# Splitting a weight load three ways, shifting small tiles and moving residual adds to the matrix engine in a fused attention and MLP forward and backward kernel

## The chip, the cores and the metric

The kernel runs on one core of one Trainium2 chip. The metric is the device time of one execution in microseconds (us). The kernel before took 856.96 us as the median of three runs (855.38 to 858.51). PE is the matrix engine, DVE the vector engine, ACT the scalar engine, POOL GpSimd, and SP the engine whose in-order queue issues the transfers (DMA). "Clock" is the granted clock of PE as a share of full speed.

## The reference, cut to what matters

```python
def reference(A_x, A_wqkv, A_wo, B_w1, B_w3, B_w2, B_x, grad_out):
    # h  = x + linear_attention(layernorm(x)) @ wo;  h2 = h + (silu(n @ w1) * (n @ w3)) @ w2, n = layernorm(h)
    # x: (1, 2048, 640) bf16, 32 heads of 20, hidden width 1728
    ...
    phi = lambda t: jnp.where(t > 0, t + 1, jnp.exp(t)) + 1e-6
    pq, pk = phi(q), phi(k)
    kv = jnp.einsum("bhsd,bhse->bhde", pk, v)
    z = jnp.einsum("bhsd->bhd", pk)
    num = jnp.einsum("bhqd,bhde->bhqe", pq, kv)
    den = jnp.einsum("bhqd,bhd->bhq", pq, z)[..., None] + 1e-6
    o = num / den
    ...
    _out, _vjp = jax.vjp(_f, A_x, A_wqkv, A_wo, B_w1, B_w3, B_w2)
    return (out, *grads)     # the output and six gradients
```

Of the kernel before, what the change touches and what calls it, by code (L numbers as in the profile page):

```python
# [9 lines left out]
P = 128  # L10
# [8 lines left out]
S, D, H, F = 2048, 640, 32, 1728  # L19
# [3 lines left out]
ST, DT, CT = S // P, D // P, CP // P  # L23
FT, FP = 14, 1792
FL = F - 13 * P
W, SC, TPC = 512, 4, 4
# [40 lines left out]
def kernel(  # L67
# [112 lines left out]
    def load_x(a, b):  # L180
        dma(out=x_sb[:, a:b, :], in_=xS[:, a:b, :])
# [35 lines left out]
    def load_pqT(c):  # L217
        dmaT(out=pqT[:, :, c * W:(c + 1) * W], in_=pq_d[c * W:(c + 1) * W, :])
# [15 lines left out]
    def on_act(t):  # L234
        return t >= XT_DMA and t % 2 == 0

    def p1_norm(t):
        xn = x_sb[:, t, :]
        (ln1.norm_act if on_act(t) else ln1.norm)(xn, xn, t)
        if t >= XT_DMA:  # L240
            dmaT(out=pqT[:, :, t * P:(t + 1) * P], in_=xn)

    def p1_tr(t):
        xn = x_sb[:, t, :]
        tr = ps.tile([P, DT, P], BF16, name="tr", bufs=2)
        for c in range(DT):
            T.transpose(tr[:, c, :], xn[:, c * P:(c + 1) * P], ident[:])

        A.copy(out=pqT[:, :, t * P:(t + 1) * P], in_=tr[:])  # L249
# [6 lines left out]
    def p1_mm(t, n0):  # L256
        acc = ps.tile([P, 2, 512], F32, name="big", bufs=2)
        for j in range(2):
            p1_half(acc[:, j, 0:HD], t, n0 + j * HD)
        return acc  # L260
# [6 lines left out]
    def phi(acc, dst, then=None):  # L267

        mq, rq = (p1.tile([P, D], BF16, name=n, bufs=4) for n in ("mq", "rq"))
        A.activation(two(mq[:]), acc[:, :, 0:HD], AF.Exp)  # L270
        A.activation(two(rq[:]), acc[:, :, 0:HD], AF.Relu)

        def rest():
            V.tensor_scalar(out=mq[:], in0=mq[:], scalar1=1.0, scalar2=1e-6, op0=ALU.min, op1=ALU.add)
            V.tensor_tensor(out=dst, in0=mq[:], in1=rq[:], op=ALU.add)
            if then is not None:
                then()
        held.append(rest)

    def phi_rest():  # L280
        while held:
            held.pop(0)()
# [4 lines left out]
    def q_tile(t):  # L287
        pq = p1.tile([P, D], BF16, name="pq", bufs=4)
        phi(p1_mm(t, 0), pq[:], lambda: q_store(t, pq[:]))
# [9 lines left out]
    def ghh_chunk(n, acc):  # L299

        c, fc = divmod(n, FT)
        mm5_to(acc, w2T, fc, g2T[c])
        if n % 2 == 0:
            ghh[n // 2] = pf.tile([P, 2, W], BF16, name="ghh", bufs=4)
        A.copy(out=ghh[n // 2][:, n % 2, :], in_=acc[:])  # L305
# [5 lines left out]
    def m_part(m, tiles):  # L311
        if m not in macc:
            macc[m] = [ps.tile([P, 512], F32, name="macc", tag=("m", "tr")[m % 2], bufs=2) for _ in range(2)]
        for t in tiles:
            for j, n in enumerate((HD, HD + 1)):
                T.matmul(macc[m][j][:, 0:n], lhsT=pk_all[:, t, m * P:(m + 1) * P],  # L316
                         rhs=x_ext[:, t, j * HD:j * HD + n], start=(t == 0), stop=(t == ST - 1))

    def m_end(m):
        mb = mbs[:, m % 4, :]  # L320
        acc = macc.pop(m)
        for j in range(2):
            A.copy(out=mb[:, j * HD:(j + 1) * HD], in_=acc[j][:, 0:HD])
        V.tensor_copy(out=Z[:, m:m + 1], in_=acc[1][:, HD:HD + 1])
        dmaT(out=mT[:, :, m * P:(m + 1) * P], in_=mb)
        dma(out=m_v[:, m, :], in_=mb)

    def kv_block(m, acc):

        a, b = M_H[m]  # L330
        n = (b - a) * DH
        for c in range(DT):
            T.matmul(acc[:, 0:n], lhsT=mT[:, c, m * P:(m + 1) * P],
                     rhs=wqkv[:, c, 2 * D + a * DH:2 * D + b * DH], start=(c == 0), stop=(c == DT - 1))
        kv, mk = (x[:, m, y].rearrange("p (h e) -> p h e", e=DA)
                  for x, y in ((kvbd, slice(a * DA, b * DA)), (mask, slice(0, M_W[m]))))
        V.tensor_tensor(out=kv[:, :, 0:DH], in0=acc[:, 0:n].rearrange("p (h e) -> p h e", e=DH),
                        in1=mk[:, :, 0:DH], op=ALU.mult)
        V.tensor_scalar(out=kv[:, :, DH], in0=mk[:, :, DH], scalar1=Z[:, m:m + 1], scalar2=None, op0=ALU.mult)
# [16 lines left out]
    def load_w2T(a, b):  # L356
        dmaT(out=w2T[:, :, a:b], in_=B_w2[a:b, :])
# [12 lines left out]
    def group_out(g):  # L370
        sl = slice(g * TPC, (g + 1) * TPC)
        dma(out=pk_v[:, sl, :], in_=pk_all[:, sl, :])
        dma(out=xn_v[:, sl, :], in_=x_sb[:, sl, :])

    for t in range(ST):
        g, i = divmod(t, TPC)
        k = p1_mm(t, D)
        if t == 0:
            p1_tr(1)
        for n in stat_of.get(t, ()):  # L380
            ln1.run(x_sb, n, n + 1)
            if on_act(n):
                ln1.bias(n)
        for n in norm_of.get(t, ()):
            if not on_act(n):
                p1_norm(n)
        phi_rest()
        phi(k, pk_all[:, t, :])
        if t + 2 < XT_DMA:
            p1_tr(t + 2)  # L390
        for n in norm_of.get(t, ()):
            if on_act(n):
                p1_norm(n)
        if t in (3, 6, 9, 11):
            q_tile((3, 6, 9, 11).index(t))
        if 5 <= t < 9:
            ghh_chunk(t - 5, ps.tile([P, 2, 512], F32, name="gp", tag="big", bufs=2)[:, 0])
        if t >= 3:
            m_part(0, [t - 3])
        if t == 13:  # L400
            load_pqT(0)
        if t >= 9:
            m_part(1, [2 * (t - 9), 2 * (t - 9) + 1])
        if i == 0 and g > 0:
            group_out(g - 1)
        elif t >= 2 and trickle:
            trickle.pop(0)()
# [6 lines left out]
    def p1_kv(m):  # L414
        kv_block(m, ps.tile([P, 2, 512], F32, name="kvp", tag="big", bufs=2)[:, 0])
# [4 lines left out]
    phi_rest()  # L420
    m_part(1, (14, 15))
    m_end(1)
    load_w2T(4 * P, 8 * P)
    q_tile(5)
    phi_rest()
    q_tile(6)
# [2 lines left out]
    phi_rest()  # L429
    m_part(2, range(ST))  # L430
    m_end(2)
    load_w2T(8 * P, F)
    m_part(3, range(ST))
    m_end(3)
    p1_kv(0)
    m_part(4, range(8))
    p1_kv(1)
    m_part(4, range(8, 15))
    p1_kv(2)
    m_part(4, range(15, ST))  # L440
    m_end(4)
    ps.release()
    load_x(0, 2)
    load_x(2, 4)
    load_pqT(1)
    while trickle:
        trickle.pop(0)()

# [36 lines left out]
        A.copy(out=oT[t][:], in_=tr[:])  # L485

    def f2_at(t, tag="nd"):
        on_pe = t < TPC
        for j in range(2):
            at = ps.tile([P, 512], F32, name="at", tag=tag, bufs=2)  # L490
            xs = x_sb[:, t, j * HD:(j + 1) * HD]
            if on_pe:
                T.matmul(at[:, 0:HD], lhsT=ident[:], rhs=xs, start=True, stop=False)
            for c in range(DT):
                T.matmul(at[:, 0:HD], lhsT=oT[t][:, c, :], rhs=wo[:, c, j * HD:(j + 1) * HD],  # L495
                         start=(c == 0 and not on_pe), stop=(c == DT - 1))
            if on_pe:
                A.copy(out=xs, in_=at[:, 0:HD])
            else:
                V.tensor_tensor(out=xs, in0=at[:, 0:HD], in1=xs, op=ALU.add)  # L500
        ln2.run(x_sb, t, t + 1)
# [129 lines left out]
    def f2_at0(t):  # L631
        f2_at(t, "o2")
# [10 lines left out]
    def f2_x(t):  # L643
        load_x(t, t + 2)

    for f, t in ((q_late, 8), (q_late, 9), (q_late, 10), (f2_kv, 3), (mlp_ghh, 4), (f2_kv, 4), (f2_ndo, 0), (q_late, 11),
                 (f2_ot, 0), (f2_ndo, 1), (q_late, 12), (f2_at0, 0), (f2_ot, 1), (f2_ndo, 2), (f2_hn, 0), (q_late, 13),
                 (f2_at0, 1), (mlp_ghh, 5), (f2_ht, 0), (f2_ot, 2), (f2_ndo, 3), (f2_hn, 1), (q_late, 14), (f2_x, 4),
                 (f2_at0, 2), (f2_ht, 1), (f2_ot, 3), (f2_hn, 2), (f2_at0, 3), (q_late, 15), (f2_ht, 2), (f2_hn, 3),
                 (mlp_ghh, 6), (f2_x, 6), (f2_ht, 3), (mlp_ghh, 7)):  # L650
        f(t)
    p1.release()
# [5 lines left out]
    def sides(late):  # L658
        side = ({}, {})
        for i in range(TPC):  # L660
            k0 = 3 * i - (i == TPC - 1)
            for k, pos, f in ((k0, 0, f2_ndo), (k0, 1, f2_ot), (k0 + 2, 1, f2_at), (k0 + 3, 0, f2_hn),
                              (k0 + 3, 1, f2_ht)):
                if late and f is f2_at and i != late - 1:
                    k, pos = k + 1, 0
                side[pos].setdefault(k, []).append((f, i))
        return side
# [623 lines left out]
```

## The kernel before: the parts that the change touches

The sequence has 16 tiles of 128 rows. The kernel forms M = pk'x in five tiles (`m_part`, `m_end`), transposes each by DMA into `mT` and multiplies it by the v weights into a kv tile (`kv_block`). Then, tile by tile, come `nd` (numerator and denominator), the output o_t, its transpose oT, the product with `wo` plus the residual (`f2_at`), and after that the MLP. `w2T` is the transposed weight w2, needed by chunks of the backward product `ghh` that are used as filling. A DMA transpose is `dmaT`; all of these and the plain stores go out on one in-order queue.

```python
def load_w2T(a, b):
    dmaT(out=w2T[:, :, a:b], in_=B_w2[a:b, :])
def load_pqT(c):                                   # transposed q of four tiles
    dmaT(out=pqT[:, :, c * W:(c + 1) * W], in_=pq_d[c * W:(c + 1) * W, :])
# ...
m_end(1)
load_w2T(4 * P, 8 * P)
q_tile(5); phi_rest(); q_tile(6); phi_rest(); q_tile(7); phi_rest()
m_part(2, range(ST)); m_end(2)
load_w2T(8 * P, F)
m_part(3, range(ST)); m_end(3)
p1_kv(0)
m_part(4, range(8))
p1_kv(1)
m_part(4, range(8, 15))
p1_kv(2)
m_part(4, range(15, ST))
m_end(4)
load_x(0, 2); load_x(2, 4)
load_pqT(1)
# ...
def f2_o(t):
    o_t = pf.tile([P, D], BF16, name="o_t", bufs=2)            # stored to o_d by f2_ot
    # ...
def q_late(t):
    pq = p1.tile([P, D], BF16, name="pq", bufs=4)              # stored to pq_d at the end
    # ...
def f2_at(t, tag="nd"):
    on_pe = t < TPC                                            # TPC = 4
    for j in range(2):
        at = ps.tile([P, 512], F32, name="at", tag=tag, bufs=2)
        xs = x_sb[:, t, j * HD:(j + 1) * HD]
        if on_pe:
            T.matmul(at[:, 0:HD], lhsT=ident[:], rhs=xs, start=True, stop=False)
        for c in range(DT):
            T.matmul(at[:, 0:HD], lhsT=oT[t][:, c, :], rhs=wo[:, c, j * HD:(j + 1) * HD],
                     start=(c == 0 and not on_pe), stop=(c == DT - 1))
        if on_pe:
            A.copy(out=xs, in_=at[:, 0:HD])
        else:
            V.tensor_tensor(out=xs, in0=at[:, 0:HD], in1=xs, op=ALU.add)
```

Between the kv tiles and the MLP runs a hand-ordered "fill list" of such steps; it is shown in the diff. In it `q_late` makes a q tile, `f2_kv` a kv tile, `f2_ndo` nd and o_t, `f2_ot` oT, `f2_at0` the product with `wo`, `f2_hn` and `f2_ht` the normalised tile and its transpose, `f2_x` loads x, and `mlp_ghh` is one ghh chunk. Tiles are counted from 0; "oT(6)" is the transposed output of tile 6.

## Time and profile before

| | before |
|---|---|
| median of the first three runs | 856.96 us |
| span of the profiled run, mean clock | 856.1 us, 1.000 |
| PE busy | 832.3 us, 97% |
| last product of M tile 3 to first nd tile | 16.13 us |
| first nd tile to first MLP product | 22.79 us |
| first MLP product to first product with w2 | 54.73 us |

The three stretches at the bottom are read from the start times of PE's instructions in the trace, and are what the change can reach. They are the first, middle and last stretch.

### The profile page before, as it was taken

What the parts mean: (1) busy time and instruction counts of PE and PEld (TensorE: products, weight loads), DVE (VectorE), ACT (ScalarE), POOL (GpSimd) and SP (SyncE); (2) the same over time, 40 slices, a digit from 0 to 9 for tenths busy, and PEclk for the clock granted to TensorE, in tenths of its full rate; (3) what the DMA queues carried; (4) which work ended last, traced back from release to release, by engine and by line L of the source; (5) the groups of instructions that cost most, each with busy time, mean ns of one, the idle gap of its engine ahead of it and who ended that gap; (6) DMA issues with size and microseconds to landing.
All of it is one profiled execution on the core that took longest, in us unless ns stands there. A gap on an engine that the chain in (4) does not pass through costs nothing.

```text
span 856.1 us, 14478 instructions
## 1 busy us (share of the span) xinstructions
PE 832.3 (97%) x5711; PEld 533.1 (62%) x5711; DVE 417.9 (49%) x958; ACT 318.6 (37%) x598; POOL 33.6 (4%) x57
## 2 busy tenths in 40 slices
PE   6998898999999999999999999999999999999998
PEld 4565644455555555677777777777777777655554
DVE  7852778878778756600036565654462454300000
ACT  4873685755555566211121111122212333311111
POOL 2310000000000000001000000000000000000000
PEclk9999999999999999999999999999999999999999
DMA  9899759867456447799959999949696688666681
GB/s 278 241 299 261 200 150 231 217 190 173 129 126 180 126 152 205 206 241 214 281 115 198 201 215 199 203 94 239 145 215 139 124 211 178 145 161 161 154 173 36
DMA packets 341107, 158.55 MB, mean 185 GB/s; under 512 B 241712, under 2 KB 339760, under 8 KB 341040
## 3 DMA queue, kind: packets, MB, share of 16 engines
q1 hardware_dynamic: 312224, 144.67, 70.9%
q10 hardware_dynamic: 28816, 12.97, 8.0%
q8 instruction: 44, 0.72, 0.4%
q14 instruction: 23, 0.19, 0.1%
HBM read 48.64 MB, written 50.32 MB: 116 GB/s over the span
## 4 chain that ended last, share of the span: by engine, by line
PE 82%; DMA 9%; DVE 3%; SPq 2%; issue 2%; ACT 2%; ACTq 0%; DVEq 0%
PE job L1085 19%; PE mm L295 18%; PE ghn L849 12%; PE gxn L1218 8%; PE o L620 7%; PE gw L788 3%; PE gwo L956 3%; PE at L495 2%; DMA ggb<-gg_d 2%; PE h L906 2%; PE dkv L1165 2%; PE big L253 2%; DMA w13b<-in_B_w_dram 2%; PE macc L316 2%; DMA oT<-o_t 1%
## 5 line engine op out<-in xcount | busy, mean ns | idle before, releaser
L1085 PE MATMUL job<-gb,hnN 128*128 128x432 bf16 x640 | 117.0, 346 | 0.0
L849 PEld LDWEIGHTS <-ggb 128*128 128x128 bf16 x864 | 83.0, 98 | 32.1 <-DMA ggb<-gg_d 1.3
L295 PE MATMUL mm<-pqT,w 128*128 128x512 bf16 x405 | 96.3, 379 | 0.8 <-ACT up L568 0.8
L1085 PEld LDWEIGHTS <-hnN 128*128 128x128 bf16 x640 | 62.6, 98 | 54.1
L295 PEld LDWEIGHTS <-w 128*128 128x128 bf16 x540 | 52.4, 98 | 61.4 <-issue 1.6
L1089 ACT CAST obs<-job 128x432 bf16<-128x432 f32 (+1 forms) x60 | 29.2, 486 | 134.7 <-PE job L1085 134.7
L620 PE MATMUL o<-w,hhT 128*128 128x320 bf16 x448 | 67.5, 299 | 0.0
L849 PE MATMUL ghn<-w13a,ggb 128*128 128x320 bf16 x448 | 65.6, 299 | 0.0
L295 PE MATMUL mm<-g2T,w2T 128*128 128x512 bf16 x260 | 64.6, 379 | 0.0
L849 PE MATMUL ghn<-w13b,ggb 128*128 128x320 bf16 x416 | 63.5, 299 | 0.8 <-DMA ggb<-gg_d 0.8
L620 PEld LDWEIGHTS <-hhT 128*128 128x128 bf16 x448 | 43.8, 98 | 23.6
L788 PE MATMUL gw<-g,hb 128*128 128x320 bf16 x416 | 57.7, 299 | 0.0
L872 ACT ACTIVATE y<-wb,s,ln_rs 128x640 bf16<-128x640 f32 x32 | 29.4, 920 | 67.1 <-DVE wb L868 67.1
L305 ACT CAST ghh<-mm 128x512 bf16<-128x512 f32 x52 | 30.5, 586 | 57.0 <-PE mm L295 56.6
L788 PEld LDWEIGHTS <-hb 128*128 128x128 bf16 x416 | 40.3, 98 | 15.3
L1218 PE MATMUL gxn<-wqT,gT 128*128 128x320 bf16 x320 | 48.7, 299 | 0.0
L560 ACT ACTIVATE sig<-mm 128x512 bf16<-128x512 f32 x56 | 33.5, 599 | 29.4 <-PE mm L295 27.2
L295 PEld LDWEIGHTS <-w2T 128*128 128x128 bf16 x280 | 27.2, 98 | 26.7 <-issue 1.5
L860 ACT ACTIVATE gs<-ghn 128x640 bf16<-128x640 f32 x16 | 11.3, 704 | 86.1 <-PE ghn L849 77.7
L253 PEld LDWEIGHTS <-pqT 128*128 128x128 bf16 x320 | 31.9, 102 | 16.7 <-issue 1.8
L253 PE MATMUL big<-wqkv,pqT 128*128 128x320 bf16 x240 | 39.2, 317 | 1.6 <-ACT pqT L249 0.8
L1085 PEld LDWEIGHTS <-g 128*128 128x128 bf16 x320 | 31.2, 98 | 12.3 <-issue 0.3
(158 smaller groups left out, 1154.2 us busy)
## 6 DMA issues: line engine op xcount, KB each, us to landing
hh_d<-hhT SPq DMA_DIRECT2D x24, 256.0 KB, 2.5
gg_d<-gate SPq DMA_DIRECT2D x24, 256.0 KB, 2.5
gg_d<-up SPq DMA_DIRECT2D x24, 256.0 KB, 2.6
ggb<-gg_d SPq DMA_DIRECT2D x6, 896.0 KB, 8.0
ggb<-gg_d SPq DMA_DIRECT2D x6, 832.0 KB, 8.5
out_dram<-obs ACTq DMA_DIRECT2D x40, 108.0 KB, 2.1
ggb<-gg_d SPq DMA_DIRECT2D x2, 1728.0 KB, 13.5
x_sb<-in_A_x_dram SPq DMA_DIRECT2D x5, 640.0 KB, 8.1
```

What stands on the lines that cost most here:

```text
L253: T.matmul(acc, lhsT=pqT[:, c, t * P:(t + 1) * P], rhs=wqkv[:, c, n0:n0 + HD], start=(c == 0), stop=(c == DT - 1))
L295: T.matmul(acc[:], lhsT=w[:, c, fc * P:(fc + 1) * P], rhs=rhs[:, c, :], start=(c == 0), stop=(c == DT - 1))
L305: A.copy(out=ghh[n // 2][:, n % 2, :], in_=acc[:])
L560: A.activation(sig[:, i, :], gp[:], AF.Sigmoid)
L620: T.matmul(o2["ps"][:, 0:HD], lhsT=hhT[c][:, fc, i * P:(i + 1) * P], rhs=w2[:, fc, j * HD:(j + 1) * HD], start=(fc == 0), stop=(fc == FT - 1))
L788: T.matmul(acc[:, j, 0:HD], lhsT=hb[b][:, t, i * P:(i + 1) * P], rhs=g2[:, t, j * HD:(j + 1) * HD], start=(t == 0), stop=(t == ST - 1))
L849: T.matmul(acc[:, j, 0:HD], lhsT=ggb[t // 2][:, k, lo:lo + P], rhs=rhs[:, j * HD:(j + 1) * HD], start=(k == 0), stop=(k == NG - 1))
L872: A.activation(out=y[:], in_=wb[:], func=AF.Identity, bias=s[:, 3:4], scale=st.rs[:, t:t + 1])
L956: T.matmul(acc[m][:, j, 0:HD], lhsT=o_sb[:, t, m * P:(m + 1) * P], rhs=g_h[:, t, j * HD:(j + 1) * HD], start=(t == 0), stop=(t == ST - 1))
L1085: T.matmul(acc[:, 0:n], lhsT=lhs[:, t, m * P:(m + 1) * P], rhs=rhs(t), start=(t == 0), stop=(t == ST - 1))
L1089: A.copy(out=ob, in_=acc[:, 0:n])
L1218: T.matmul(acc[:, j, 0:HD], lhsT=g, rhs=wqT[:, k, j * HD:(j + 1) * HD], start=(k == 0), stop=(k == 14))
```

## The change

The intent: take the 512-row w2T piece out of the stretch where the M tiles have to be transposed, and put it into an earlier one; send the last piece later, when M is done; let the third kv tile run after M instead of inside it; fill one wait in the list with a ghh chunk; and, for tiles 4 to 7, let PE add the residual (an identity matmul) instead of DVE.

```diff
@@ phase 1 @@
+        if t == 11:
+            load_w2T(4 * P, 8 * P)
@@ after M tile 1 @@
-    load_w2T(4 * P, 8 * P)
@@ after M tile 2 @@
-    load_w2T(8 * P, F)
     m_part(3, range(ST))
     m_end(3)
+    load_pqT(1)
     p1_kv(0)
     m_part(4, range(8))
     p1_kv(1)
-    m_part(4, range(8, 15))
-    p1_kv(2)
-    m_part(4, range(15, ST))
+    m_part(4, range(8, ST))
     m_end(4)
     ps.release()
     load_x(0, 2)
     load_x(2, 4)
-    load_pqT(1)
+    load_w2T(8 * P, F)
@@ f2_at @@
-        on_pe = t < TPC
+        on_pe = t < 2 * TPC
@@ fill list @@
-    for f, t in ((q_late, 8), (q_late, 9), (q_late, 10), (f2_kv, 3), (mlp_ghh, 4), (f2_kv, 4), (f2_ndo, 0), (q_late, 11),
+    for f, t in ((q_late, 8), (f2_kv, 2), (q_late, 9), (q_late, 10), (f2_kv, 3), (mlp_ghh, 4), (f2_kv, 4), (f2_ndo, 0), (q_late, 11),
                  (f2_ot, 0), (f2_ndo, 1), (q_late, 12), (f2_at0, 0), (f2_ot, 1), (f2_ndo, 2), (f2_hn, 0), (q_late, 13),
-                 (f2_at0, 1), (mlp_ghh, 5), (f2_ht, 0), (f2_ot, 2), (f2_ndo, 3), (f2_hn, 1), (q_late, 14), (f2_x, 4),
-                 (f2_at0, 2), (f2_ht, 1), (f2_ot, 3), (f2_hn, 2), (f2_at0, 3), (q_late, 15), (f2_ht, 2), (f2_hn, 3),
+                 (f2_at0, 1), (f2_ot, 2), (f2_ht, 0), (f2_ndo, 3), (f2_hn, 1), (q_late, 14), (f2_x, 4), (f2_at0, 2),
+                 (f2_ot, 3), (f2_ht, 1), (mlp_ghh, 5), (f2_hn, 2), (f2_at0, 3), (q_late, 15), (f2_ht, 2), (f2_hn, 3),
                  (mlp_ghh, 6), (f2_x, 6), (f2_ht, 3), (mlp_ghh, 7)):
```

As in the prediction, A is the moved loads and kv tiles, B the order of the fill list, C the identity matmul.

## The prediction

> **What bounds the kernel now.** I read the page first, then the busy time of the engines by stretch, then the waits of the matrix engine, then the order of time around each wait, with the DMA queue's own instructions.
>
> ```profile
> span 856.1 us, 14478 instructions
> ...
> PE 832.3 (97%) x5711; PEld 533.1 (62%) x5711; DVE 417.9 (49%) x958; ACT 318.6 (37%) x598; POOL 33.6 (4%) x57
> ```
>
> PE is busy 97% of the span, so anything that does not shorten PE's list of work or its 24 us of idle time is worth nothing. The stretches say where that idle time lies (columns: span, then busy time of PE, PEld, DVE, ACT, POOL, then clock, DMA share, GB/s):
>
> ```profile
> 63.00:72.00 9.00, 9.00 (x70) 6.43 (x68) 1.32 (x4) 2.28 (x5) 0.00 (x0) 1.00 1.07 308
> 72.00:80.00 8.00, 5.04 (x44) 3.57 (x42) 0.99 (x5) 0.53 (x2) 0.00 (x0) 1.00 1.08 226
> 80.00:86.00 6.00, 5.52 (x43) 3.69 (x41) 3.22 (x10) 4.92 (x14) 0.00 (x0) 1.00 1.01 210
> 86.00:92.00 6.00, 4.73 (x44) 3.11 (x42) 3.48 (x14) 2.92 (x7) 0.00 (x0) 1.00 0.91 196
> 92.00:103.00 11.00, 11.00 (x102) 8.21 (x99) 9.17 (x30) 8.79 (x23) 1.09 (x2) 1.00 0.62 192
> 103.00:110.00 7.00, 5.57 (x43) 3.37 (x41) 4.23 (x13) 5.06 (x12) 1.28 (x2) 1.00 0.50 152
> ...
> 118.00:130.00 12.00, 12.00 (x68) 6.34 (x69) 11.58 (x25) 7.95 (x16) 0.93 (x1) 1.00 0.76 213
> 130.00:142.00 12.00, 10.36 (x57) 4.80 (x54) 11.62 (x29) 7.33 (x14) 0.93 (x1) 1.00 1.00 236
> 142.00:154.00 12.00, 10.56 (x55) 5.31 (x56) 8.90 (x19) 5.91 (x12) 0.93 (x1) 1.00 1.00 244
> ```
>
> PE idle: 2.96, 0.48, 1.27 us (sum 4.7, the end of M and the kv tiles), 1.43 us (the fill list), 1.64 and 1.44 us (first block of the MLP), and 0.30 in 110 to 118: 9.5 us. This is all the change can reach; from 160 to 400 us PE shows no idle time.
>
> ```profile
> PE kvp L333 <- DMA mT<-mbs: 3.0, 1, 3.0
> PE at L495 <- DMA oT<-o_t: 2.5, 3, 1.6
> ...
> PE at L495 <- ACT oT L485: 1.0, 1, 1.0
> PE mm L333 <- DMA mT<-mbs: 0.9, 1, 0.9
> PE mm L295 <- ACT up L568: 0.8, 2, 0.7
> ```
>
> The order of time shows why the third transposed M tile is late: it is ready for transposing at 68.1 us, but the queue that issues it is in order and first spends 3.36 us on a w2T piece and then three stores:
>
> ```profile
> 68.70 1.24 SPq L325 DMA_TRANSPOSE mT<-mbs  x1
> 69.99 0.56 SPq L326 DMA_DIRECT2D m_d<-mbs  x1
> 70.60 3.36 SPq L357 DMA_TRANSPOSE w2T<-in_B_w_dram  x1
> ...
> 74.07 1.50 SPq L285 DMA_DIRECT2D pq_d<-pq  x3
> ...
> 75.65 1.64 SPq L325 DMA_TRANSPOSE mT<-mbs  x1
> ...
> 77.96 4.19 SPq L357 DMA_TRANSPOSE w2T<-in_B_w_dram  x1
> 79.59 0.32 PEld L333 LDWEIGHTS <-mT 128*128 128x128 bf16 x5 [3.30 <-DMA mT<-mbs]
> ```
>
> The fourth M tile then waits behind the last w2T piece and goes out at 82.25, the fifth at 84.34; the last kv tile starts at 87.39.
>
> **What the Trainium skill says.** "TensorE: Matmul & The Clock Gate", section "Wait — 56ns, not 53.3ns?": warm matmuls start N/2.4 GHz plus about 2.5 ns apart. For 320 columns that is 135.8 ns, for 512 it is 215.7; the chain has ten 320-column matmuls in 1.36 us and five 512-column ones in 1.08 us, so it agrees, and 136 ns, not the mean duration of 299 ns, is the price of one matmul. "DMA: Bandwidth & Descriptors", section "Issuing engines are not separate DMA queues": all transfers share 16 engines. The DMA share of 1.01 to 1.08 from 63 to 86 us agrees that moving a transfer there moves work and removes none. The same page, "Latency and other measured facts", gives 261 GB/s for a DMA transpose; 655 KB would then take 2.5 us (an estimate from that page). The three w2T pieces landed 5.4, 6.3 and 12.5 us after issue, in a full queue. "PSUM — Partial Sum Buffer", section "The four PSUM rules", says that a seed other than zero should be put through PE by an identity matmul; that is how tiles 0 to 3 already do it (no trace shows the rule).
>
> **The change, part by part.**
>
> *Part A, w2T and the kv tiles.* It takes one w2T piece (640 KB) out of the queue between the second and third M tile and puts it at t=11, about 50 us; the last piece and the third kv tile go later, and the load of transposed q for tiles 4 to 7 goes ahead of the fifth M tile. Gain if all else stood still: the waits of 2.96, 0.48 and 0.90 us, 4.3 us in all. But at 50 us the DMA engines are full too (1.03 to 1.16 in 48 to 58 us), so everything behind it moves by the piece's own time: 2.5 us by the page's rate, with about 1 us of empty engines that I see at 60.6 to 61.6 before a transpose, 3.3 us as my estimate. The first M tile was issued at 63.29 and landed 8.3 us later, at 71.6, just as PE finished M(3) at 71.85. Moved by 3.3 us it lands near 74.9, and the first kv tile waits about 3 us, which it does not now. From there: 0.35 (kv 0), 8 x 2 matmuls of 137 ns each 2.2 and kv 1 gives 77.5; second half of M(4) 2.2, 79.9; q tile 8 with 1.36, 81.2; kv 2; two q tiles 2.7 and kv 3, 84.7; one 5-matmul chunk 1.08, so the last kv tile at about 85.9 against 87.39. Its M tile, no longer behind a w2T piece but behind the 3.65 us issue of transposed q, should land near 84 to 85. Gain 1.5 us in this working, 3 to 4 if the shift is below 1 us. I take 1.8.
>
> *Part B, the fill list.* The 1.08 us chunk 5 moves into the place where PE waited 1.01 us for the copy of oT(3). In front it leaves a hole: transposes of tile 2 come up right after the output tile, while DVE delivers o_t(2) at 97.7 and hn(0) at 98.1 and PE is there at 97.4, so about 0.6 us is lost. But the chain afterwards is DVE's (o_t(3) ready at 101.6, hn(1) at 102.0, unchanged), so PE is on time for it, and about 0.6 to 0.7 us is won by 104.3. I take 0.7.
>
> *Part C, identity matmul for tiles 4 to 7.* Added: 4 tiles x 2 halves x 136 ns = 1.09 us of PE. Removed: 8 DVE adds, about 0.44 us apart in the order of time, 3.5 us of DVE. Added to ACT: 8 copies of 0.43 us, 3.4 us. DVE is 97% busy from 118 to 142 us, ACT about 65%, so the load goes to the right engine. What does that win? PE's waits there (0.30, 0.16, 1.55, 0.69, 0.68 us) are for transposes and stores issued late; some stand behind DVE products, others behind a 4.45 us transpose issue and full DMA engines. I expect them to shrink by 0.9 us of 3.4, and the identity matmul at the head of a group needs no oT and can use part of the wait. Net: 1.1 lost, 0.9 to 1.0 won; -0.1.
>
> Sum: 1.8 + 0.7 - 0.1 = 2.4 us. From 856.96 that is 854.5. From 154 to 388 us PE is the bound with no wait, and the later loads are released by PE's progress, so I expect it to be passed on to the end.
>
> **The rivals.** First: the full gain of A (4.3), B (1.0) and C (PE waits fall by 3, less 1.1): 7.2 us, 849.8. For it: each wait stands in the trace. Against it: full DMA engines on both sides of the move. Second: the wait merely changes place, A and B give nothing, C costs its 1.1 us: 858. For it: the first M tile has less than 0.3 us of slack. Against it: four transposes go out earlier by up to 4 us, and no w2T piece stands between them. Third: the start gains, but the stage of 388 to 425 us, where the chain runs over weight transposes of 10 and 13.6 us, takes it back: 857. Against it: PE is idle 0.45 us in all of 400 to 500. A large loss would need ACT to become the bound by 3.4 us; at 65% it should not.
>
> **Range and chances.** The point is 854.5. The low end, 850.8, is nearly the first rival; the high end, 857.5, is no gain and a little noise (the three runs of before span 3.1 us). Two per cent is 17.1 us, more than all 9.5 us of reachable idle time, so faster by over 2% has a chance of 0.01, slower by over 2% 0.01, within 0.98.
>
> **What would show it.** Right: at the first kv tile a new PE wait of 2 to 3 us for mT, at the third none; the last kv tile at 84 to 87 us; no wait of 1.0 us for the oT copy near 104; eight more 320-column matmuls against the identity, DVE adds into x_sb 16 instead of 24, and DVE below 97% in 118 to 142. Wrong: no wait at the first kv tile (A worth 3 us more), a wait at the last kv tile behind the load of transposed q (A worth nothing), PE waiting for ACT evictions in 118 to 154 (C negative), or a lead at 150 us that is gone at 430.

## More of the kernel before

Profile lines of before are in the prediction; one more reading turned out to matter. It is the order of time of SP's queue (start, duration, operation, out<-in, count):

```profile
88.24 3.80 SPq L218 DMA_TRANSPOSE pqT<-pq_d  x1
92.13 2.00 SPq L285 DMA_DIRECT2D pq_d<-pq  x4
94.19 0.44 SPq L480 DMA_DIRECT2D o_d<-o_t  x1
```

Four stores of q tiles and the first store of an output tile stand in line behind a transposed load, and go out only from 92.13 us on. Keep this time in mind.

## The result, and the profile after

The changed kernel took 859.72 us (median of four runs, 858.56 to 860.26) beside 856.73 us for before (four runs, 855.38 to 858.51). The ratio is 1.0032, 95% interval 1.001 to 1.0053; a ratio here is the mean time of one kernel's fast runs over that of the other's of the same rounds, so not quite the ratio of the medians quoted. It lies within 2%, as predicted, but outside the predicted range and on the wrong side: 2.4 us of gain was expected.

From the page of the changed kernel (the eight added matmuls are there, x5719 for x5711, and eight DVE instructions less, x950 for x958):

```profile
span 858.5 us, 14494 instructions
...
PE 833.5 (97%) x5719; PEld 533.2 (62%) x5719; DVE 415.0 (48%) x950; ACT 322.0 (38%) x606; POOL 33.5 (4%) x57
```

PE's own order of time, at the four places that matter (the bracket is the idle time before the instruction and what ended it):

```profile
74.31 0.48 PE L333 MATMUL kvp<-wqkv,mT 128*128 128x140 bf16 x5 [3.16 <-DMA mT<-mbs]
...
86.11 0.48 PE L333 MATMUL mm<-wqkv,mT 128*128 128x140 bf16 x5 [0.60 <-DMA mT<-mbs]
...
98.20 0.68 PE L482 MATMUL tr<-ident,o_t 128*128 128x128 bf16 x5 [1.89 <-DVE o_t L469]
...
143.31 0.85 PE L494 MATMUL at<-wo,oT 128*128 128x320 bf16 x5 [2.18 <-DMA oT<-o_t]
```

The first kv tile waits 3.16 us, as part A says (about 3), and the last one starts at 86.11 (85.9 said). The second agreement is luck in part: this run reached the last product of M tile 3 by 0.72 us earlier than before (70.86 us for 71.58). Counted from there the last kv tile starts after 15.25 us, where the prediction has 14.3 and before 15.81; of the 0.9 us over the prediction, 0.60 is the wait for its own M tile, in the second line above. PE reaches the first nd tile 1.28 us ahead of before, those 0.72 us included. Then come two waits that the prediction does not have in this size. The first has its cause on the DMA queue:

```profile
49.15 5.49 SPq L357 DMA_TRANSPOSE w2T<-in_B_w_dram  x1
...
66.17 3.06 SPq L325 DMA_TRANSPOSE mT<-mbs  x1
...
86.37 5.18 SPq L357 DMA_TRANSPOSE w2T<-in_B_w_dram  x1
91.65 1.98 SPq L285 DMA_DIRECT2D pq_d<-pq  x4
93.68 0.45 SPq L479 DMA_DIRECT2D o_d<-o_t  x1
```

and shows on DVE, which may not write a buffer again before it is stored:

```profile
94.04 0.49 DVE L513 TENSOR_TENSOR pq<-mq,rq 128x640 bf16<-128x640 bf16 x1 [2.12 <-DMA pq_d<-pq]
...
97.59 0.89 DVE L469 TENSOR_TENSOR o_t<-nd,rden 128x380 bf16<-128x380 f32 x2 [1.28 <-DMA o_d<-o_t]
```

The stores go out at 91.65 us where they went out at 92.13 before. PE came 1.28 us earlier and the stores only 0.48, since the last w2T piece (5.18 us on the queue) now stands where the transposed q (3.80 us) stood. DVE waits, o_t(2) comes late, PE waits 1.89 us for it, and the lead is gone.

The second wait, 2.18 us for oT(6), is followed by a fall of the clock. Stretches of 2 us of the changed kernel (columns: span, then busy time of PE, PEld, DVE, ACT, POOL, then clock, DMA share, GB/s):

```profile
142.00:144.00 2.00, 0.69 (x5) 0.51 (x6) 0.30 (x1) 0.41 (x1) 0.00 (x0) 1.00 0.56 124
144.00:146.00 2.00, 2.00 (x11) 1.07 (x9) 0.00 (x0) 0.43 (x1) 0.00 (x0) 0.64 0.99 266
146.00:148.00 2.00, 2.00 (x6) 0.65 (x5) 1.41 (x5) 1.40 (x4) 0.09 (x1) 0.50 0.90 251
```

The same stretches of before, which has the waits in smaller parts:

```profile
144.00:146.00 2.00, 1.76 (x9) 0.69 (x7) 1.90 (x7) 0.19 (x1) 0.56 (x1) 1.00 0.69 173
146.00:148.00 2.00, 1.55 (x8) 0.72 (x8) 1.04 (x2) 2.00 (x5) 0.36 (x1) 1.00 0.85 204
```

PE is "busy" 2.00 of 2.00 in the changed kernel, but with 6 matmuls instead of 8: the clock column 0.50 is what to look at. The clock record of the trace has this half-speed period 3.4 us long, which costs 1.7 us.

In the last stretch alone the changed kernel loses 1.6 us against before (56.32 for 54.73), in the middle 1.3 (24.08 for 22.79), and wins 0.6 in the first (15.57 for 16.13). Nothing later differs by the change: from the start of the w2 products to the end the time is 685.9 to 691.5 us whatever the kernel (to the start of PE's last instruction), and its spread comes from one transfer-bound stage of the backward pass (145.7 to 151.3 us by chance). That stage, and the clock, make single runs of one kernel in the same rounds differ by up to 7.2 us in before and 9.5 us in e13_bufswarm.

### The profile page after: what moved, and what is told of

The parts are those of the page before. It is cut to its first block, busy times and chain, and to the rows that moved or that the text cites. A ratio compares the mean times of both kernels' runs of the same rounds, so it can differ in the third digit from the quotient of the medians.

```text
span 858.5 us, 14494 instructions
## 1 busy us (share of the span) xinstructions
PE 833.5 (97%) x5719; PEld 533.2 (62%) x5719; DVE 415.0 (48%) x950; ACT 322.0 (38%) x606; POOL 33.5 (4%) x57
## 4 chain that ended last, share of the span: by engine, by line
PE 82%; DMA 3%; DVE 1%; ACT 1%; issue 0%; ACTq 0%; SPq 0%; DVEq 0%
PE mm L295 19%; PE job L1084 18%; PE ghn L848 11%; PE gxn L1217 8%; PE o L619 7%; PE gw L787 7%; PE gwo L955 3%; PE at L494 2%; PE h L905 2%; PE dkv L1164 2%; DMA ggb<-gg_d 1%; DMA oT<-o_t 1%; DMA xnT<-xn_d 1%; PE h L936 1%; PE gkv L928 1%; PE nd L456 0%
## 5 line engine op out<-in xcount | busy, mean ns | idle before, releaser
L1217 PEld LDWEIGHTS <-gT 128*128 128x128 bf16 x320 | 31.2, 98 | 12.5 <-DMA gT<-g_k 0.4
L1084 PEld LDWEIGHTS <-g 128*128 128x128 bf16 x320 | 31.2, 98 | 12.3 <-issue 0.3
```

What stands on the lines that cost most here:

```text
L1084: T.matmul(acc[:, 0:n], lhsT=lhs[:, t, m * P:(m + 1) * P], rhs=rhs(t), start=(t == 0), stop=(t == ST - 1))
L1217: T.matmul(acc[:, j, 0:HD], lhsT=g, rhs=wqT[:, k, j * HD:(j + 1) * HD], start=(k == 0), stop=(k == 14))
```

## The experiments

Theory at the outset: the wait for the stores behind the last w2T piece takes back A and B, and C's one long wait loses the clock. Rivals: C itself costs its 1.1 us of matmuls; A moves work into a full queue and gains nothing; or the 3 us were the chance of the runs.

The table has all of them. "Clock" is the mean over the timed runs (six of each kernel; four in the first measure; 55 of before); one half-speed period of 3.4 us makes it 0.0020 less. The three stretches and the last column, where the clock fell, are of the one profiled run; a fall at the very end, after PE's last matmuls, is in every trace and left out.

| kernel | ratio to before (95%) | clock | first | middle | last | half speed at |
|---|---|---|---|---|---|---|
| before | | 0.9983 | 16.13 | 22.79 | 54.73 | |
| r_before (before again) | 0.9981 (0.9954 to 1.0008) | 0.9983 | 15.49 | 22.80 | 54.84 | |
| the change, first measure | 1.0032 (1.001 to 1.0053) | 0.9968 | 15.57 | 24.08 | 56.32 | oT(6) |
| r_after | 1.0008 (0.998 to 1.0036) | 0.9968 | 15.18 | 24.44 | 54.46 | |
| r2_after | 1.0005 (0.9983 to 1.0026) | 0.9965 | 16.26 | 21.91 | 55.92 | first kv |
| e1_A | 1.0011 (0.9987 to 1.0034) | 0.9967 | 16.73 | 22.80 | 53.69 | first kv, later once |
| e2_AB | 1.0001 (0.9976 to 1.0026) | 0.9972 | 17.67 | 21.86 | 53.67 | first kv, twice as long |
| e3_C | 1.0003 (0.9977 to 1.0029) | 0.9975 | 16.30 | 22.79 | 56.47 | third kv, oT(6) |
| e4_B | 0.9983 (0.9959 to 1.0006) | 0.9985 | 17.33 | 21.77 | 54.30 | |
| e5_warm | 1.0015 (0.9986 to 1.0043) | 0.9977 | 15.01 | 27.01 | 54.00 | o_t(2) |
| e6_late | 0.9994 (0.9968 to 1.0019) | 0.9980 | 16.56 | 21.61 | 54.52 | first kv |
| e7_spread | 0.9985 (0.9958 to 1.0011) | 0.9980 | 10.39 | 24.34 | 58.77 | start, oT(4) |
| e8_front | 0.995 (0.9923 to 0.9977) | 0.9992 | 11.23 | 23.73 | 54.53 | |
| e9_ABwarm | 0.9995 (0.9964 to 1.0025) | 0.9987 | 14.98 | 23.00 | 55.97 | oT(6) |
| e10_latewarm | 0.9994 (0.9969 to 1.0019) | 0.9977 | 15.06 | 21.61 | 57.14 | oT(6) |
| e11_frontC | 0.9981 (0.9959 to 1.0003) | 0.9990 | 11.70 | 24.14 | 55.39 | |
| e12_bufs | 1.0032 (1.0012 to 1.0052) | 0.9960 | 17.73 | 21.97 | 54.86 | first kv, twice as long |
| e13_bufswarm | 1.0009 (0.9979 to 1.0038) | 0.9977 | 16.52 | 21.98 | 54.33 | first kv |
| e14_afterwarm | 1.0003 (0.998 to 1.0026) | 0.9990 | 14.66 | 23.44 | 52.47 | |
| e15_bufskvwarm | 0.9991 (0.9972 to 1.001) | 0.9995 | 15.19 | 21.97 | 52.94 | |

(In e7, e8 and e11 a ghh chunk of 1.08 us moved from the first stretch into the middle one.)

### The parts alone: e1_A, e2_AB, e3_C, e4_B

e1_A is the change with the old end of the list and without C; e2_AB the change without C; e3_C the kernel before with C alone; e4_B the kernel before with the list's new order (the third kv tile staying where it was).

```diff
# e1_A against the change: list order undone, and
-        on_pe = t < 2 * TPC
+        on_pe = t < TPC
# e2_AB against the change: the same line only
# e3_C against before
-        on_pe = t < TPC
+        on_pe = t < 2 * TPC
# e4_B against before
-                 (f2_at0, 1), (mlp_ghh, 5), (f2_ht, 0), (f2_ot, 2), (f2_ndo, 3), (f2_hn, 1), (q_late, 14), (f2_x, 4),
-                 (f2_at0, 2), (f2_ht, 1), (f2_ot, 3), (f2_hn, 2), (f2_at0, 3), (q_late, 15), (f2_ht, 2), (f2_hn, 3),
+                 (f2_at0, 1), (f2_ot, 2), (f2_ht, 0), (f2_ndo, 3), (f2_hn, 1), (q_late, 14), (f2_x, 4), (f2_at0, 2),
+                 (f2_ot, 3), (f2_ht, 1), (mlp_ghh, 5), (f2_hn, 2), (f2_at0, 3), (q_late, 15), (f2_ht, 2), (f2_hn, 3),
```

> Part A alone: the three loads moved and the third kv tile in the fill list, the fill list otherwise as before, identity matmul for tiles 0 to 3 only. My theory: the lead at the last kv tile is about 1 us (first kv tile waits about 3 us, third none), then the last w2T piece holds back the stores of o_t and pq for 5 us, DVE waits 2 to 3 us for their buffers near 93 to 98 us, and the lead at the first MLP matmul is 0 to 0.7 us; end 856 to 857 against 856.7. Rival (the fill list order makes the DVE wait): no DVE wait for o_d or pq_d stores, lead 1.3 us or more kept to the end, 855.3.

> Parts A and B, without C. My theory (C loses 1.6 us by its matmuls and a clock drop, A and B are zero in sum): 856.5 to 857.3, a PE wait of about 1.9 us for o_t(2) near 96 to 98, clock 1.00 in the first block of the MLP. Rival (A and B themselves lose): 858 or more.

> Part C alone: identity matmuls for tiles 4 to 7. My theory: 1.1 us of PE added, waits for oT shorter by about 0.8 us, and a clock drop where the wait for oT(6) passes 2 us, worth 1.7 us: 857.5 to 859, with granted clock below 1 between 140 and 150. Rival (only the added matmuls cost, the clock drop is chance): 857 to 857.5 and clock 1.00.

> Part B alone: the order of the fill list, with the third kv tile and the loads where they were. My theory: with no w2T piece in front of the stores, o_t(2) comes on time, the wait for it is below 0.8 us, the wait of 1.0 us for the oT copy is gone, end 856.0 to 856.6. Rival (the order itself makes the hole): wait of 1.5 us or more for o_t(2), 857.5 to 858.

Measured (medians): 859.63, 859.24, 859.41 and 858.32 us beside 858.96 for before. No part is told from zero by the times. The traces say more. B alone shortens the middle stretch by 1.0 us (21.77 for 22.79), as predicted; its place without A has no lead to lose at the stores. A alone did not shorten the first stretch, because in both kernels with A the clock fell at the first kv tile, for 3.4 us in e1_A and 6.8 in e2_AB. And e2_AB, which has A and B together, showed no wait of PE for o_t(2) at all: PE came so late that of the stores only one still held DVE up (1.2 us, for pq). So the two losses shut each other out, which no sum of parts would show.

### Repeats, and the two suspects one by one: r_after, e5_warm, e6_late, e7_spread

r_after is the changed kernel again. e5_warm puts twelve idle matmuls (their result is overwritten; 1.6 us) ahead of the one that waits for oT(6), so that the clock should hold. e6_late is the change without C and with the last w2T piece at the end of the list. e7_spread takes both later w2T pieces out of the M stretch and sends them as smaller ones between the stores.

```diff
# e5_warm against the change
+            for _ in range(12 if (t, j) == (6, 0) else 0):
+                T.matmul(at[:, 0:HD], lhsT=ident[:], rhs=xs, start=True, stop=True)
# e6_late against e2_AB
-    load_w2T(8 * P, F)
-                 (mlp_ghh, 6), (f2_x, 6), (f2_ht, 3), (mlp_ghh, 7)):
+                 (mlp_ghh, 6), (f2_w, 0), (f2_x, 6), (f2_ht, 3), (mlp_ghh, 7)):     # f2_w loads that piece
# e7_spread against e2_AB (cut)
-            load_w2T(4 * P, 8 * P)
-    load_pqT(1)
-    load_w2T(8 * P, F)
+    # in the list: four loads of 128 rows, one after each of (f2_ndo, 0), (q_late, 12), (f2_hn, 1), (f2_hn, 2);
+    # load_pqT(1) after (q_late, 15); the rest in two loads after (mlp_ghh, 6) and (mlp_ghh, 7)
```

> The changed kernel once more, on the same chip and in the same rounds as the next three. My theory: first kv tile waits about 3 us, o_t(2) about 1.9 us unless the clock dropped before it, oT(6) about 2.2 us; 1 to 3 us above before. The clock drop is a matter of how free-running windows of 3.4 us fall on the waits (in the six traces so far a window dropped the clock where PE was busy for 0.38 of it or less and not where it was 0.44 or more), so here it may fall elsewhere; a window of 0.44 or more followed by a drop, or one of 0.38 or less without, would be against this theory.

> The changed kernel with 12 idle identity matmuls (1.6 us of PE, results overwritten) ahead of the output tile 6, in the place where PE waits for oT(6). My theory: the wait shrinks from 2.2 to about 0.6 us, the clock never drops at 140 to 150, and the stretch from the first MLP matmul to the first down projection takes 54.6 us or less, against 56.3 in the changed kernel; time about 1 us lower on average. Rival (the drop has nothing to do with that wait): drop at 140 to 150 as before, and the 1.6 us is added: 57.9 us for the stretch.

> Parts A and B without C, and the last w2T piece issued at the end of the fill list instead of ahead of the first stores. My theory: no DVE wait for stores of pq or o_t over 0.5 us, no PE wait for o_t(2) over 0.8 us, and 22.0 us or less from the first nd matmul to the first MLP matmul whether or not the clock dropped before it (24.1 in the changed kernel, 22.8 before). Rival (the order of the list is to blame): 23.5 to 24.

> A candidate to beat both: B and the moved kv tiles, no C; the second w2T piece out of the full stretch altogether, as four pieces of one chunk each between the stores of the fill list, the third in two pieces at its end, transposed q for tiles 4 to 7 after them. My theory: no wait over 0.7 us at any kv tile, first nd matmul 4 to 5 us earlier after M(3) than before (16.1 us from the end of M(3) in before, so 11 to 12), 21.5 to 22.5 us from there to the first MLP matmul, no clock drop up to 130 us; time 2 to 5 us under before. Rival (the queue or DMA ends the waits elsewhere): the fill list grows by as much as the kv tiles win, time within 1 us of before.

Measured: 858.42, 860.21, 857.59 and 857.18 us beside 858.17. The repeat, in other rounds, lies 0.1% above before, so part of the first 0.3% may have been chance (the two intervals overlap). In r_after the first stretch is again 15.2, the middle again long, 24.44, and the last one, with no fall of the clock, 54.46: the middle loss is not chance, the last one is partly. e5_warm kept the clock at oT(6) and its 1.6 us of idle matmuls made the last stretch no longer (54.00), but now the clock fell in the 3.1 us wait for o_t(2), which made the middle one 27.01; its time gained nothing. e6_late has 21.61 in the middle, yet PE was late there by a fall of the clock at the first kv tile, so it proves less than hoped. e7_spread wins 5.7 us in the first stretch, 1.1 of it the moved chunk, and loses it behind a transposed q that goes out too late for the MLP (PE waits 1.86 us for it), a wait of 2.43 us for oT(4) and the fall of the clock after that.

### The better order, and twins with the clock held: r_before, e8_front, e9_ABwarm, e10_latewarm

r_before is the kernel before under a new name. e8_front is e7 with the transposed q back in the M stretch and the w2T pieces moved forward. e9_ABwarm and e10_latewarm are e2_AB and e6_late with twenty idle matmuls (2.7 us) inside the wait at the first kv tile, so that the clock cannot fall there. Between these two, the twins, only the place of the last w2T piece differs.

```diff
# e9_ABwarm against e2_AB, and the same in e10_latewarm against e6_late
+        acc = ps.tile([P, 2, 512], F32, name="kvp", tag="big", bufs=2)[:, 0]
+        for _ in range(20 if m == 0 else 0):
+            T.matmul(acc[:, 0:HD], lhsT=ident[:], rhs=x_sb[:, 0, 0:HD], start=True, stop=True)
+        kv_block(m, acc)
# e8_front against before (cut)
-    load_w2T(4 * P, 8 * P)
-    load_w2T(8 * P, F)
     m_end(3)
+    load_pqT(1)
     # third kv tile out of M(4) into the list, as in the change; new order of the list:
+    for f, t in ((q_late, 8), (f2_kv, 2), (q_late, 9), (q_late, 10), (f2_kv, 3), (f2_kv, 4), (f2_ndo, 0), (f2_w, 4), (f2_w, 5),
+                 (q_late, 11), (f2_ot, 0), (f2_ndo, 1), (q_late, 12), (f2_w, 6), (mlp_ghh, 4), (f2_at0, 0), (f2_ot, 1),
+                 (f2_w, 7), (f2_ndo, 2), (f2_hn, 0), (q_late, 13), (f2_at0, 1), (f2_ot, 2), (f2_ht, 0), (f2_ndo, 3), (f2_hn, 1),
+                 (f2_w3, 8), ... (f2_hn, 2), (f2_w3, 11), ...                # f2_w: 128 rows, f2_w3: up to 384 rows of w2T
```

> The kernel before, once more under its own label, for a second trace of it and to see how far two labels of the same program lie apart: ratio within 0.2% of 1; from the end of M(3) to the first nd 16.1 us, from there to the first MLP matmul 22.8, from there to the first down projection 54.7, each within 0.5 us unless the clock drops, which adds 1.7.

> The spread candidate mended: transposed q for tiles 4 to 7 ahead of the fifth M tile (the queue stood idle there), the w2T pieces as early in the fill list as the queue is free, nothing of w2T after the list. My theory: 10.4 us from the end of M(3) to the first nd, 23 us from there to the first MLP matmul (one chunk of 1.08 us has moved into it), 54 us to the first down projection, 87.4 us in sum against 93.7 before; time 4 to 6.5 us under before. Rival (what is won in front is given back at transposes in the first MLP block): sum 90 or more, time less than 3 us under before.

> A and B without C, with 20 idle matmuls in the place of the wait at the first kv tile, so that the clock can't drop there. My theory (the last w2T piece ahead of the stores is what takes the lead back): wait of 1.5 us or more for o_t(2) with DVE waiting on stores of pq or o_t, 23.8 to 24.4 us from the first nd to the first MLP matmul, as in the changed kernel. Rival: 22 us or less, as in A and B with the drop.

> The same with the last w2T piece at the end of the fill list. My theory: no DVE wait on stores, no wait for o_t(2) over 0.8 us, 21.5 to 22 us from the first nd to the first MLP matmul, so 2 us or more below its twin; time about 1.5 to 2 us below its twin. Rival: no difference between the twins.

Measured: 855.9, 853.72, 857.87 and 858.11 us beside 857.45. The same program under another name gave 0.9981, interval 0.9954 to 1.0008, so two tenths of a per cent is what chance can do here. The twins: e9_ABwarm waits for a store and has 23.00 in the middle (lines of its waits: total, times, longest); e10_latewarm has neither wait and 21.61.

```profile
DVE o_t L472 <- DMA o_d<-o_t: 1.0, 1, 1.0
...
PE tr L485 <- DVE o_t L472: 0.8, 1, 0.8
```

That is 1.4 us for the place of one transfer, though the wait of PE itself was smaller than I had in mind. Both lost the clock at oT(6) afterwards, without C, so C is not needed for that. In the first stretch both have about 15.0.

e8_front beats before: 853.72 us (853.01 to 854.47), ratio 0.995; r_before, in the same rounds, had 855.9. The change was not in these rounds, but none of its three intervals reaches down to that of e8. Its queue shows how (order of time of SP):

```profile
77.09 2.60 SPq L218 DMA_TRANSPOSE pqT<-pq_d  x1
...
84.26 2.86 SPq L357 DMA_TRANSPOSE w2T<-in_B_w_dram  x2
87.21 0.52 SPq L285 DMA_DIRECT2D pq_d<-pq  x1
```

Three q tiles are stored from 82.77 on, ahead of two small pieces of w2T (2.86 us together, not 5.18 in one), so the next stores go out at 87.21 where the change's went at 91.65; and no M tile waits behind a weight. The three stretches sum to 89.49 us, 4.2 less than before (87.4 was expected). Nearly all of it is in the first: 11.23 us, or 12.3 with the moved chunk, for 16.13. Which of e8's moves does it was not separated.

### C on the better order, and more buffers: r2_after, e11_frontC, e12_bufs, e13_bufswarm

r2_after is the change once more. e11_frontC is e8_front with C. e12_bufs is the change with one more buffer for pq and a place of its own for o_t(2), so that neither has to wait for a store; e13_bufswarm is that with e5's idle matmuls.

```diff
# e11_frontC against e8_front
-        on_pe = t < TPC
+        on_pe = t < 2 * TPC
# e12_bufs against the change (the first edit at both places)
-        pq = p1.tile([P, D], BF16, name="pq", bufs=4)
+        pq = p1.tile([P, D], BF16, name="pq", bufs=5)
-        o_t = pf.tile([P, D], BF16, name="o_t", bufs=2)
+        o_t = p1.tile([P, D], BF16, name="o_x") if t == 2 else pf.tile([P, D], BF16, name="o_t", bufs=2)
# e13_bufswarm: e12_bufs with the two lines of e5_warm
```

> The changed kernel a third time, as the twin of the next two in the same rounds. My theory: 24.1 to 24.4 us from the first nd to the first MLP matmul, with DVE waiting on stores of pq and o_t; from M(3) to the first nd 15.2 to 15.6 (16.9 to 17.3 if the clock drops there, and then no wait for o_t); ratio to before 1.000 to 1.003.

> The faster candidate (w2T pieces out of the M stretch and between the stores) with C added, that is the identity matmul for tiles 4 to 7. My theory: C by itself is worth nothing, within 0.5 us, unless the clock drops at oT(6): 54 to 55 us from the first MLP matmul to the first down projection (54.5 without C), 56 to 57 with a drop; time 853 to 856. Rival (DVE relief pays once the front is early): 53.5 us or less and a time below 853.

> The changed kernel with one more buffer for pq (5 for 4) and one of its own for o_t of tile 2; loads, list and matmuls as in the change. My theory (the moved w2T piece hurts because DVE waits for buffers whose stores stand behind it): no DVE wait on stores, no wait for o_t(2) over 0.8 us, 21.7 to 22.3 us from the first nd to the first MLP matmul; time 0 to 2 us under its twin, as the wait for oT(6) takes part of the lead. Rival (PE is held there by DVE's own work or by the order): 23.5 to 24.5.

> The same with the 12 idle matmuls ahead of output tile 6. My theory: as above, and no clock drop between 140 and 150 us; from the first MLP matmul to the first down projection 55 us or less; time 1 to 2.5 us under the changed kernel, about that of before or 1 us under it. Rival: the clock drops there all the same, or the idle matmuls lengthen the stretch to 56 or more.

Measured: 858.07, 856.46, 860.03 and 858.26 us beside 857.99. The buffers were inconclusive: the clock fell at the first kv tile in all three kernels with that wait, so r2_after was late too, PE had no wait for o_t(2) in it (21.91; DVE still waited 1.2 us for a store of pq), and there was nothing for the buffers to win. C on the better order made the last stretch 0.9 us longer in one look (55.39 for 54.53), and e11's ratio is 0.9981 where e8's was 0.995 in the batch before; that pair alone would make C a loss, but the means over all traces, further down, do not.

How the fall looks: r2_after, stretches of 2 us after the wait at the first kv tile,

```profile
74.00:76.00 2.00, 1.63 (x13) 1.18 (x14) 0.45 (x2) 0.00 (x0) 0.00 (x0) 0.88 1.13 361
76.00:78.00 2.00, 2.00 (x9) 1.17 (x8) 0.00 (x0) 0.00 (x0) 0.00 (x0) 0.50 1.06 321
```

and e14_afterwarm (next), the same instructions with the wait filled:

```profile
74.00:76.00 2.00, 1.70 (x16) 1.10 (x14) 0.40 (x2) 0.00 (x0) 0.00 (x0) 1.00 1.13 333
76.00:78.00 2.00, 2.00 (x20) 1.49 (x18) 0.06 (x1) 0.00 (x0) 0.00 (x0) 1.00 1.76 332
```

20 matmuls of M tile 4 in 2 us against 9.

### The buffers again with the clock held: e14_afterwarm, e15_bufskvwarm

e14_afterwarm is the whole change with e9's idle matmuls ahead of the first kv tile; e15_bufskvwarm is that with e12's buffers. They differ by the buffers alone. (The twenty idle matmuls take 2.88 us in e14's trace, not the 1.3 us of the expectation.)

> The change whole, with 20 idle identity matmuls (about 1.3 us of PE) ahead of the first kv tile, inside a wait of about 3 us, so that the clock stays whole there. Theory (the last w2T piece holds up the stores that free the buffers of pq and o_t): PE comes early to the first nd tile, DVE waits together 2 to 3.5 us for pq_d and o_d to be stored, PE waits 0.8 to 2 us for o_t(2), and first nd to first MLP matmul takes 22.9 to 24.4 us. Rival (the long middle stretch of the first measure was chance): 21.6 to 22.3 us with no wait for a store over 0.5 us. Whole time 856 to 860 in both.

> The same with a fifth buffer of pq and a place of its own for o_t(2), so that no DVE instruction there waits for a store behind the last w2T piece. Theory: no wait of DVE for pq_d or o_d over 0.3 us, no wait of PE for o_t(2) over 0.4, and 21.5 to 22.3 us from first nd to first MLP matmul, 1 to 2 us below its twin. Rival: the wait goes over to the transposed q of the tiles or to some other product behind the piece, and the stretch stays within 0.5 us of its twin's. Whole time: theory 1 us below the twin at most, which the spread of the times may hide.

Measured: 857.35 and 856.7 us beside 857.48. DVE in e14_afterwarm:

```profile
93.63 0.49 DVE L516 TENSOR_TENSOR pq<-mq,rq 128x640 bf16<-128x640 bf16 x1 [1.79 <-DMA pq_d<-pq]
...
96.88 0.89 DVE L472 TENSOR_TENSOR o_t<-nd,rden 128x380 bf16<-128x380 f32 x2 [0.98 <-DMA o_d<-o_t]
```

SP and DVE in e15_bufskvwarm:

```profile
85.80 6.70 SPq L357 DMA_TRANSPOSE w2T<-in_B_w_dram  x1
92.60 2.71 SPq L285 DMA_DIRECT2D pq_d<-pq  x4
```

```profile
92.40 0.49 DVE L516 TENSOR_TENSOR pq<-mq,rq 128x640 bf16<-128x640 bf16 x1
...
95.08 0.89 DVE L472 TENSOR_TENSOR o_x<-nd,rden 128x380 bf16<-128x380 f32 x2
```

In e15 the stores are even later (92.60), but nobody waits for them: no bracket stands behind these two lines, o_t(2) is written 1.8 us earlier, PE's wait of 1.3 us for it is gone and the middle stretch is 21.97 instead of 23.44. With e9 and e10 this settles what the middle loss is: the buffers' wait for stores behind the last w2T piece, worth 1.5 us in this pair of traces. The times do not tell the twins apart; the interval of each is wider than that.

### What the clock cost in all runs

Every timed run records its mean clock, so the fall can be counted without a trace. Of the 52 runs of kernels whose wait at the first kv tile was open (the change 16, e1, e2, e5, e6, e12, e13), 4 had a clock of 0.999 or more; of the 24 runs with that wait filled (e9, e10, e14, e15), 14; of the 55 of before, 20. The change's mean is 0.9967 over 16 runs, before's 0.9983 over 55: 1.66 against 0.87 half-speed periods to a run, if 0.0020 is one. In r_after and r2_after, against before of the same rounds, the time lost to the clock (its deficit times the run's length) is 0.77 and 2.06 us, mean 1.4. With that taken out their times are 0.0 us above and 2.0 us below before, on average 1.0 below (standard error about 0.6). That the change shortens the work is not shown by this: r_before, which is the same program as before, comes out 1.2 us below in the same way, and the first measure 1.4 us above (an estimate, with the clock 0.9983 for before, as that of its own runs isn't on record).

When does it fall? In the traces the half-speed periods are 3.4 us long (twice 6.8), and they lie whole multiples of 3.413 us after the first full-speed grant or after one another (39 of them after the first grant in the change, 19 between the two in e3, 114 between the two in e1). "TensorE: Matmul & The Clock Gate" in the Trainium skill, section "What's actually happening", has such a free-running window of 3413 ns, and that agrees. If I lay these windows over PE's busy time in all 20 traces, every window at full speed, from the kernel's start-up to its end, in which PE was busy up to 38% was followed by half speed, and of those from 40% up only one, a start-up window at 45% in e7. (In the two double periods, e2 and e12, a window at half speed was followed by another although PE was busy for 63% and 70% of it; the rule does not cover that.) So a wait of some 2 to 3.4 us loses 1.7 us or not, by how the window lies over it, which differs from run to run. An estimate from these figures: if a window falls when 62% of its 3.41 us, 2.12 us, are idle, and may lie anywhere, a lone wait of 2.87 us (the old one at the third kv tile, mean of four traces) is hit in 0.60 of the runs, one of 3.29 us (the new one at the first, mean of nine) in 0.72, and one of 2.2 us in about 0.4.

## Why the prediction was wrong, point by point

In short, two steps failed. A's new wait at the first kv tile was priced at its length, without the half-speed period that followed it in 6 of 9 traces. And B's chain, taken as fixed by DVE's own work, was held by stores behind the moved w2T piece, 1.4 and 1.5 us in the two pairs of twins.

**The bound and the place.** Right: only the first 9.5 us of idle time moved, the later time does not depend on the change, and within 2% was right.

**Part A, predicted +1.8 us.** The waits came where the working has them, but the price of one step was wrong. The first M tile's transpose went out 3.6 us later, counted from the last product of M tile 3 (3.3 estimated). The new wait came as said (3.16 us; "about 3 us"), the third kv tile had none, and the last started at 86.11 (85.9 said, by the early start of that run). Over seven traces with the clock whole at that wait (the change, r_after, e5, e9, e10, e14, e15) the first stretch averages 15.09 us against 16.32 for the three traces of the old order with the clock whole (before, r_before, e4): +1.2, or +0.7 without e4, whose 17.33 holds a wait of 1.78 us at the last kv tile. In the six traces where the clock fell there it averages 16.91: -0.6. Over all traces, fallen or not and without idle matmuls at that wait, it is 16.31 in the old order (four) and 16.36 in the new (nine): nothing. The step that failed is "the first kv tile waits about 3 us, which it does not now", counted at the length of the wait alone. In 6 of the 9 traces with that wait open it cost 1.7 us or more on top. The old wait of 2.96 us at the third kv tile has the same risk, and e3 fell into it, but it was 1 of 4 traces. Whether it really falls less often there isn't shown: by the estimate above the two waits are hit in 0.60 and 0.72 of the runs, and 1 of 4 against 6 of 9 can be chance.

**Part B, predicted +0.7 us.** Right by itself: e4_B +1.0, and 21.6 to 22.0 us in every kernel with B where no store was in the way. Wrong in the place where the change puts it: with A's lead and the clock whole, the middle stretch is 24.08, 24.44, 23.44 and 23.00 (the change, r_after, e14, e9), mean 23.74, so -0.95. The step that failed is "But the chain afterwards is DVE's (o_t(3) ready at 101.6, hn(1) at 102.0, unchanged)". I took DVE's chain as fixed by DVE's own work. It was held by stores, through four pq and two o_t buffers, and the stores by the last w2T piece, which I had only followed up to its own issue. e15 against e14 and e10 against e9 show it: 1.5 and 1.4 us.

**Part C, predicted -0.1 us.** Not contradicted, and not settled. Its signs came: the eight matmuls more, eight DVE instructions less, and DVE busy for 93% of 118 to 142 us instead of 97. The last stretch without a fall of the clock and without idle matmuls averages 54.34 us in six traces with C (r_after, r2_after, e11, e12, e14, e15) and 54.33 in seven without (before, r_before, e1, e2, e4, e6, e8); single ones spread over 1 to 3.5 us, so no pair shows it. PE waits in it for 2.1 us on average instead of 3.1, near the "0.9 to 1.0 won". But both averages hang on e14 and e15, whose wait for oT(6) was short for a reason not found; the other four with C average 55.16 us, 0.8 longer than without. Not foreseen: with C these waits become one, for oT(6), of up to 2.5 us, long enough for the clock to fall, as it did in the first measure. That is not C's alone: without C a single wait for oT(6) was 2.75 us in e4, 2.55 in e8, 3.14 in e9 and 2.85 in e10, and in the last two the clock fell.

**The sum.** With the clock whole: 1.2 - 0.95 + 0 = +0.25 us (-0.25 without e4). With it falling at the first kv tile: -0.6, and since PE is then late for the stores, 22.79 - 21.9 = +0.9, together +0.3. Either way near nothing, instead of 2.4, before the second fall at oT(6), which takes 1.7 in some runs. So the second rival ("the wait merely changes place", 858) was near in result, and right in its terms only in part: A gives something where the clock holds, B where no store is in the way, and C's cost is between nothing and 0.8 us. The first measure's 1.0032 is above what the traces account for; the two repeats, 1.0008 and 1.0005, fit them. The cause of the rest stays open; the spread of runs is a guess.

**What stays open.** Whether the change is truly slower than before: three measures give 1.0005 to 1.0032, two with intervals across one. Why oT(6)'s wait was only 0.30 and 0.78 us in e14 and e15 and 1.55 to 2.5 in the other kernels with C (without idle matmuls ahead of it), which is why their last stretch is short. What differs in the traces is the transfer: that transpose landed 3.65 and 3.69 us after its issue there, 3.18 in before, and 5.07 to 5.48 in the change, its two repeats, e3, e11, e12 and e13. And what the better order would be with buffers and C together, which was not run.

## What to carry to other kernels

Before you move a large transfer on an in-order queue to a "free" place, list the small stores that will stand behind it and the buffers that they free: a piece moved out of one chain's way may land in another's, and the one order here that gained, 0.5% (e8_front), took the weight out of the M stretch and sent it in small pieces between the stores; the parts of that were not measured apart. A gap of 2 to 3 us on PE should be priced at its length plus the risk of 1.7 us at half clock; several short gaps or a filled one are cheaper than one long one. (The first stretch averages 14.97 us in the four traces with the gap filled and 16.36 in the nine with it open; the times of the runs do not show that gain.) And when a change is worth less than one such period, compare the recorded clock of the runs along with the time, because the median of four runs can't see it.

## What the Trainium skill lacked or had wrong

- "TensorE: Matmul & The Clock Gate", section "HAM oscillation — how this bites in real kernels", gives as the rule "no PE-idle gaps >~3.4µs." Here a gap of 2.18 us (0.25 us more just before it) was enough for 3.4 us at half clock, and so were the 2.97 us in r2_after. The share of busy time in a window decides: up to 38% the clock fell, from 40% up it held after all full-speed windows but one.
- The same section offers another loop order or more rows against this, but not to fill the wait. Twenty idle identity matmuls inside the wait did it in all four traces with them (no fall at the first kv tile), and 14 of 24 runs had a clock of at least 0.999, for 4 of 52 with the wait open.
- "DMA: Bandwidth & Descriptors" has a transfer rate for a DMA transpose (section "Latency and other measured facts"), but on how long one holds the queue it is issued on I found only cycle counts in a table about trn3 and earlier chips, and no time by size for trn2. Here that is what counted: 1.2 us for most pieces of 128 rows, 2.50 to 9.25 us for 512 rows, 3.88 to 6.70 us for the 704 rows of the last w2T piece, and the stores behind it waited that long.
